# Expert stage of an attention-and-experts kernel: row numbers in one read, placements together, fetches ahead of the dense stores

## The chip, the cores and the metric

The kernel runs on one core of one Trainium2 chip. Its time is the device time of one execution in microseconds (us). Before the change three runs gave 252.63, 248.10 and 251.63; their median is 251.63.

## The reference

Block-sparse attention is followed by a mixture of experts on its result. What the last stage must compute:

```python
x = attn_out.transpose(0, 2, 1, 3).reshape(B * S, H * D)   # 3072 tokens x 512
y_dense = np.maximum(x @ w1_dense, 0.0) @ w2_dense
logits = x @ w_gate                                          # 8 experts
expert_idx = np.argmax(logits, axis=1)
...
gate_w = probs[np.arange(N), expert_idx]
for e in range(E):
    mask = expert_idx == e
    h = np.maximum(x[mask] @ w1[e], 0.0)
    y_moe[mask] = gate_w[mask, None] * (h @ w2[e])
return y_dense + y_moe
```

There are 4 batches of 8 heads with 768 positions, so 3072 tokens; each token goes to the one expert with the largest logit, and every token also gets the dense product.

## The kernel before

The attention part takes two heads at a time over 16 steps. When a batch of 768 tokens is done, `batch_fills` makes its later work: transposes (`xtr`), the logits and gate weights (`gate`), each token's slot (`ranks`), the placement of the tokens (`place`), and the dense product in 28 pieces (`l1` and `l2`). For the first three batches this is spread between the attention steps of the next batch. The last batch has no attention behind it, so its pieces are spread by hand over the first blocks of the expert stage.

Placing means that GpSimd (POOL) writes 128 tokens, each as a row of 544 two-byte values (the token, its gate weight and its number), into the DRAM tensor `table` at the rows that `ranks` found: six indirect DMAs for a batch (line 360). `table` has a range of rows for each expert, so a block of 128 tokens of one expert is 128 rows in sequence.

There are two lists of blocks. The first (N1 = 11 blocks, 0 to 10) is made when three batches are counted and holds only tokens of these. The second (20 blocks, 11 to 30) is made by `lists` after the last batch is counted, and holds the rest. A list gives each block its expert (`eo`, an offset into the weights) and its first row in `table` (`ro`). Both are read into registers by `registers` (line 435): SyncE (SP) needs `ro` to fetch rows, TensorE (PE) and VectorE (DVE) need `eo` to find the weights. The last three blocks are under a condition and are rarely run, so the loop goes over 28 blocks (0 to 27).

For a block the work is:

- `fetch` (line 456): SP reads 128 rows of `table` into a tile `xg`; there are 14 such tiles, so a fetch from block 14 on waits until the block 14 earlier has been used up, its scatter included.
- `own` (line 471): DVE copies the expert's first weights out of a big tile.
- `tx` (lines 815 and 817): PE transposes the rows, DVE copies them out of PSUM.
- `e1` (lines 824 and 827): the first product, and ScalarE (ACT) applies the ReLU.
- `e2` (lines 845, 852, 853): the second product, ACT multiplies by the gate weight into one of five tiles `yo`, and POOL adds it to the output rows with an indirect DMA. Here it is called the block's scatter. For block 27 POOL reads the dense rows first (`dense_rows`, line 837), DVE adds, and the scatter writes the sum.

The dense product's results are stored to the output by SP in two halves for every 128 tokens (line 403). A scatter must come after the dense store of the same tokens. For blocks of the first list the kernel declares that they hold no token of the last batch, so their scatters wait only for the earlier batches' dense stores; the scatters from block 11 on wait for all of them.

Each engine works its instructions off in order. In what order the instructions of one engine stand is decided by the order in the code and by a scheduler; `tc.issue_after` asks that something be put behind a given instruction. SP's queue of the last stage holds fetches, dense stores, the reads of `ro`, and `empty`: eight writes of zero rows behind each expert's tokens (line 868), whose row numbers are read at line 864.

In the loop, `extra` says which pieces of the last batch are made at which block: `gate` and `ranks` at block 0, placement t at block 1 + t, the clearing writes at block 3, the 28 dense pieces over blocks 1 to 9. `AHEAD` and `READY` bound how far fetches are asked for ahead: the first list's as soon as eight ahead, the second's three for each block from block 8 on, each behind the latest dense store that has been issued.

Of the kernel before, what the change touches and what calls it, by code (L numbers as in the profile page):

```python
# [17 lines left out]
def kernel(  # L18
# [14 lines left out]
    NT = S // 128  # L33
# [9 lines left out]
    NBLK = NM + E - 1  # L43
# [13 lines left out]
    N1 = (N * (B - 1) // B - E * 127 + 127) // 128  # L57
# [41 lines left out]
    latest = {}  # L99
# [53 lines left out]
    N1R = -(-N1 // 4) * 4  # L153
# [77 lines left out]
    def apart(dma, group, reason):  # L231

        if group in groups:
            tc.declare_no_dep(dma.ins, group=group, reason=reason)
        groups.add(group)
        tc.add_to_no_dep_group(group, dma.ins)
# [195 lines left out]
    rows = []  # L432

    def registers(src, engine, top, why):
        _, v = nc.values_load_multi_w_load_instructions(src, engines=[engine], min_val=0, max_val=top,  # L435
                                                        skip_runtime_bounds_check_because=why,
                                                        bass_reorder=False)
        return v

    def load_offs():  # L440

        k = len(offs)
        n, c = (min(4, N1 - k), k) if k < N1 else (min(10, NBLK - k), k - N1 + N1R)
        for have, engine in ((offs, mybir.EngineType.PE), (offs1, mybir.EngineType.DVE)):
            have.extend(registers(eo[:, c : c + n], engine, (E - 1) * NK * 512,
                                  "the expert of a block is at most the last"))

    def load_rows(n):
        rows.extend(registers(ro[:, len(rows) : n], mybir.EngineType.SP, EMPTY,
                              "blocks lie in their expert's rows, or are the empty one"))  # L450
# [3 lines left out]
    def fetch(i):  # L454
        es[i]["x"] = xg = eg.tile([128, XW], U16, name="xg")
        ld = nc.sync.dma_start(out=xg, in_=table[bass.ds(rows[i], 128)])
        if i < N1:
            tc.add_to_no_dep_group("full", ld.ins)
# [5 lines left out]
    def own(i):  # L464
        if i < 1:
            w = eg.tile([128, NK, 512], HF, name="w1a", bufs=1)
        else:
            w = later[0].tile([128, NK, 512], HF, name="w1", bufs=2)
        es[i]["w1"] = w
        with tc.issue_after(latest["xT"].ins) if "xT" in latest else nullcontext():  # L470
            nc.vector.tensor_copy(w.rearrange("p j f -> p (j f)"), w1f[:, bass.ds(offs1[i], NK * 512)])  # L471

    FIRST = 6
    with (
# [251 lines left out]
        for i, (p, u) in enumerate(seq):  # L726
# [59 lines left out]
            if p == NP - 2 and u == 8:  # L786
                load_rows(N1)
                load_offs()
# [9 lines left out]
    with (  # L798
# [8 lines left out]
        a, d, ranks, places, _ = batch_fills(B - 1)  # L807
# [3 lines left out]
        def tx(i):  # L811
            s = es[i]
            tp = p1.tile([128, NK, 128], HF, name="tp", tag="tr")
            for ko in range(NK):
                nc.tensor.transpose(tp[:, ko], s["x"][:, ko * 128 : (ko + 1) * 128].bitcast(HF), ident)  # L815
            s["xT"] = xT = et.tile([128, NK, 128], HF, name="exT")
            latest["xT"] = nc.vector.tensor_copy(xT, tp)  # L817

        def e1(i):
            s = es[i]  # L820
            hp = p2.tile([128, NK, 128], FP, name="hp", tag="h")
            for j in range(NK):
                for ko in range(NK):
                    nc.tensor.matmul(hp[:, j], s["w1"][:, ko, j * 128 : (j + 1) * 128], s["xT"][:, ko],  # L824
                                     start=(ko == 0), stop=(ko == NK - 1), skip_group_check=True)
            s["hT"] = h = et.tile([128, NK, 128], HF, name="ehT")
            nc.scalar.activation(h, hp, AF.Relu)  # L827

        def tokens(i):
            return bass.IndirectOffsetOnAxis(ap=es[i]["x"][:, Dm + 2 : Dm + 4].bitcast(mybir.dt.int32), axis=0)  # L830

        def dense_rows(i):

            es[i]["dense"] = dr = et.tile([128, Dm], FP, name="dr", bufs=1)
            nc.gpsimd.memset(dr, 0.0)
            with tc.issue_after(latest["pool"].ins):
                ga = nc.gpsimd.indirect_dma_start(out=dr, out_offset=None, in_=out, in_offset=tokens(i),
                                                  bounds_check=N - 1, oob_is_err=False)
            apart(ga, "add", "every token is in one block")

        def e2(i):
            s = es[i]
            yp = p3.tile([128, Dm], FP, name="yp", tag="y")
            for j in range(NK):
                nc.tensor.matmul(yp, s["hT"][:, j], w2f[:, bass.ds(offs[i] + j * 512, 512)],  # L845
                                 start=(j == 0), stop=(j == NK - 1))
            o = et.tile([128, Dm], FP, name="yo", bufs=5)
            gate, to = s["x"][:, Dm : Dm + 2].bitcast(FP), tokens(i)
            if "dense" in s:
                nc.vector.scalar_tensor_tensor(o, yp, gate, s["dense"], ALU.mult, ALU.add)  # L850
            else:
                nc.scalar.mul(o, yp, gate)  # L852
            sc = nc.gpsimd.indirect_dma_start(out=out, out_offset=to, in_=o, in_offset=None, bounds_check=N - 1,  # L853
                                              oob_is_err=False,
                                              compute_op=ALU.bypass if "dense" in s else ALU.add)
            latest["pool"] = sc
            apart(sc, "add", "every token is in one block")
            if i < N1:
                tc.declare_no_dep(sc.ins, group="dense", reason="the first blocks hold no token of the last batch")
                tc.add_to_no_dep_group("add1", sc.ins)  # L860
# [9 lines left out]
                tc.declare_no_dep(z.ins, group="full", reason="the first blocks end before these rows")  # L870

        AHEAD = 8
        READY = 8
        for i in range(1, 1):
            own(i)
        tx(0)
        extra = {0: a[:NT] + [a[NT], ranks], **{1 + t: [f] for t, f in enumerate(places)}}
        extra[3].append(empty)
        for n, f in enumerate(d):
            extra.setdefault(1 + n * (N1 - 2) // len(d), []).append(f)  # L880
        got = FIRST

        RARE = 3
        NOFT = NBLK - RARE
        for i in range(NOFT):
            if i > 2 and len(rows) < NBLK:
                load_rows(min(len(rows) + 4, NBLK))
            while got < min(i + AHEAD + 1, NOFT, N1 + 3 * max(i - READY + 1, 0)):
                if got < N1:
                    fetch(got)  # L890
                else:
                    with tc.issue_after(latest["ys"].ins):
                        fetch(got)
                got += 1
            if 1 <= i + 1 < NOFT:
                own(i + 1)
            e1(i)
            if i + 1 < NOFT:
                tx(i + 1)
            for f in extra.get(i, ()):  # L900
                f()
            if i > 0:
                e2(i - 1)
            if len(offs) < min(i + 4, NBLK):
                load_offs()
            if i == NOFT - 6:
                dense_rows(NOFT - 1)
            if i == READY + 1:
                total = nc.values_load_multi_w_load_instructions(
                    nblk, min_val=0, max_val=N2, bass_reorder=False,  # L910
                    skip_runtime_bounds_check_because="the blocks that are left are at most N2")[1][0]
# [39 lines left out]
```

## Time and profile before

| | us |
|---|---|
| median of the three runs | 251.63 |
| lowest and highest | 248.10, 252.63 |
| the profiled execution, its own time | 250.08 |
| its span | 248.4 |
| PE busy (share of the span) | 207.8 (84%) |
| DVE busy | 176.2 (71%) |
| ACT busy | 174.4 (70%) |
| POOL busy | 161.6 (65%) |

The mean granted clock of PE is 0.984. In the profile, "q" behind an engine's name is its sequencer, which waits, branches, reads registers and issues DMAs; these are not counted as busy. Times in the timeline count from the span's start. In a row of the timeline stand the start, the length, the engine, the line, the operation, the output and inputs by name, the number of instructions merged, and in brackets the idle time before it with what ended it. A wait for several things is put down to the one that came last by the profile; where that had long been done, it was another. The last 7.5 us are the last scatter and the end of the program, so what matters in this stage is when the last scatter can start.

### The profile page before, as it was taken

To read this page: it belongs to the slowest core of one execution; us is meant where nothing else is said; L and a number is where in the kernel's file an instruction comes from. 1 tells how busy PE (TensorE), PEld (TensorE's weight loads), DVE (VectorE), ACT (ScalarE), POOL (GpSimd) and SP (SyncE) were. 2 spreads that over 40 slices of the span, in tenths; PEclk is the share of its full clock that TensorE was granted. 3 is DMA by queue.
4 is the path that set the end of the run, shared out by engine and by line. 5 is a ranking of instruction groups with operands and counts; after the bars stand their busy time and mean duration, and the time that the engine had idled before them with its cause. 6 is when DMAs were issued, how large, how long until landed. Compare 5 with 4: busy or idle time off the path is not lost. (4 is left out here: it accounts for less than half of the span.)

```text
span 248.4 us, 7579 instructions
## 1 busy us (share of the span) xinstructions
PE 207.8 (84%) x2771; PEld 148.7 (60%) x2771; DVE 176.2 (71%) x555; ACT 174.4 (70%) x325; POOL 161.6 (65%) x199
## 2 busy tenths in 40 slices
PE   1688878888998999988999998989999869979930
PEld 0466555666665676756667765667666557757710
DVE  3889999989989789797798998588423135545410
ACT  5589788878787898696899787815656636646620
POOL 6457997586289677268977427603888543888881
PEclk9999999999999999999999999999999999999985
DMA  7999999999999999989999966167599999977785
GB/s 181 252 254 253 208 226 255 253 205 261 226 180 348 192 295 233 203 176 222 304 190 256 222 116 180 62 163 213 123 267 210 162 245 228 195 133 102 123 118 104
DMA packets 75446, 50.54 MB, mean 204 GB/s; under 512 B 29712, under 2 KB 68496, under 8 KB 75408
## 3 DMA queue, kind: packets, MB, share of 16 engines
q1 hardware_dynamic: 60176, 30.72, 48.1%
q0 software_dynamic: 15232, 19.32, 46.5%
q8 instruction: 23, 0.38, 0.6%
q14 instruction: 15, 0.12, 0.2%
HBM read 41.93 MB, written 18.23 MB: 242 GB/s over the span
## 5 line engine op out<-in xcount | busy, mean ns | idle before, releaser
L567 ACT ACTIVATE ex<-sp 128x512 f16<-128x512 f32 (+1 forms) x176 | 91.5, 607 | 10.5 <-PE sp L563 8.1
L563 PE MATMUL sp<-rT,kT 128*128 128x128 f16 (+3 forms) x384 | 63.9, 261 | 3.6 <-ACT ex L567 1.2
L853 POOL DMA_INDIRECT out_dram<-yo,xg x28 | 44.8, 1600 | 26.0 <-DMA xg<-table 13.1
L569 POOL TENSOR_SCALAR_AFFINE_SELECT ex<-ex 128x512 f16<-128x512 f16 x48 | 32.3, 686 | 34.9 <-ACT ex L567 32.2
L582 PE MATMUL op<-v,ex 128*128 128x65 f16 x672 | 45.5, 194 | 7.4 <-POOL ex L569 5.3
L582 PEld LDWEIGHTS <-ex 128*128 128x128 f16 x672 | 35.6, 98 | 22.5 <-POOL ex L569 9.7
L817 DVE COPY exT<-tp 128x512 f16<-128x512 f16 x28 | 11.9, 424 | 33.2 <-PE tp L815 27.4
L563 PEld LDWEIGHTS <-kT 128*128 128x128 f16 x384 | 28.3, 98 | 7.4 <-issue 4.4
L824 PEld LDWEIGHTS <-w 128*128 128x128 f16 x432 | 26.3, 98 | 8.2 <-issue 2.9
L360 POOL DMA_INDIRECT table<-xbig,slot x24 | 24.9, 1038 | 9.4 <-issue 9.1
L824 PE MATMUL hp<-exT,w 128*128 128x128 f16 x432 | 29.2, 219 | 1.8 <-issue 1.8
L852 ACT ACTIVATE yo<-yp,xg 128x512 f32<-128x512 f32 x27 | 18.6, 687 | 15.0 <-PE yp L845 14.6
L845 PE MATMUL yp<-we,ehT 128*128 x112 | 28.9, 379 | 0.3 <-ACT ys L400 0.2
L379 PE MATMUL hp<-xT,wd 128*128 128x384 f16 x128 | 28.6, 325 | 0.6 <-DVE xT L248 0.6
L505 DVE TENSOR_REDUCE ks<-kp 128x24 f16<-128x768 f16 x28 | 25.5, 946 | 3.7 <-ACT kp L501 3.5
L827 ACT ACTIVATE ehT<-hp 128x512 f16<-128x512 f32 x28 | 16.7, 597 | 14.8 <-PE hp L824 11.3
L395 PE MATMUL yp<-wd,hT 128*128 128x512 f16 x96 | 25.9, 379 | 0.3
L384 ACT ACTIVATE hT<-hp 128x384 f16<-128x384 f32 x30 | 15.0, 499 | 9.5 <-PE hp L379 9.0
L471 DVE COPY w<-we 128x2048 f16 x27 | 19.5, 724 | 1.8 <-PE hp L824 1.7
L593 DVE TENSOR_TENSOR xbig<-op,rs 128x384 f16<-128x384 f32 x32 | 17.5, 548 | 0.9 <-DVE rs L591 0.7
L400 ACT COPY ys<-yp 128x512 f32<-128x512 f32 x21 | 12.8, 607 | 6.2 <-PE yp L395 6.2
L493 POOL CAST v<-vf 128x768 f16<-128x768 f32 x16 | 13.4, 840 | 4.2 <-DMA vf<-in_v_dram 3.0
(149 smaller groups left out, 364.1 us busy)
## 6 DMA issues: line engine op xcount, KB each, us to landing
we<-in_moe_w_dram POOLq DMA_DIRECT2D x16, 512.0 KB, 7.7
kf<-in_k_dram SPq DMA_DIRECT2D x32, 192.0 KB
qf<-in_q_dram SPq DMA_DIRECT2D x32, 192.0 KB
vf<-in_v_dram SPq DMA_DIRECT2D x32, 192.0 KB
out_dram<-ys SPq DMA_DIRECT2D x48, 128.0 KB
xg<-table SPq DMA_DIRECT2D x28, 136.0 KB
table<-zt SPq DMA_DIRECT2D x9, 136.0 KB
wd<-in_moe_w_dense_dram POOLq DMA_DIRECT2D x2, 512.0 KB, 8.8
```

What stands on the lines that cost most here:

```text
L360: sc = nc.gpsimd.indirect_dma_start(out=table, out_offset=bass.IndirectOffsetOnAxis(ap=keep["slot"][:, t : t + 1], axis=0), in_=xbig[b % 2 ...
L379: nc.tensor.matmul(hp, wd[:, ko, j * 128 : (j + 1) * 128], xT[:, ko, g * G * 128 : (g + 1) * G * 128], start=(ko == 0), stop=(ko == NK - 1))
L395: nc.tensor.matmul(yp, hold["h"][:, j, i * 128 : (i + 1) * 128], wd[:, NK + j], start=(j == 0), stop=(j == NK - 1))
L471: nc.vector.tensor_copy(w.rearrange("p j f -> p (j f)"), w1f[:, bass.ds(offs1[i], NK * 512)])
L505: nc.vector.tensor_reduce(out=ks[:, i], in_=kp.rearrange("d (c w) -> d c w", w=32), op=op, axis=mybir.AxisListType.X)
L563: last = nc.tensor.matmul(sp[:, o : o + w], kT[p % NB][g][:, kt * 128 : (kt + 1) * 128], rT[p % NB][g][:, a * 128 : z * 128], start=(o == ...
L567: scored.append((last, nc.scalar.activation(ex[:, 0:o], sp[:, 0:o], AF.Exp, scale=-0.125)))
L569: latest["pool"] = nc.gpsimd.affine_select(out=ex, in_=ex, compare_op=ALU.is_ge, fill=0.0, base=0, pattern=[[0, 4], [1, 2], [2, 64]], chan ...
L582: nc.tensor.matmul(s["op", g][:, t * (D + 1) : (t + 1) * (D + 1)], ex[:, o : o + 128], v16[p % NB][:, g, kt, :], start=first, stop=(last_o ...
L824: nc.tensor.matmul(hp[:, j], s["w1"][:, ko, j * 128 : (j + 1) * 128], s["xT"][:, ko], start=(ko == 0), stop=(ko == NK - 1), skip_group_che ...
L845: nc.tensor.matmul(yp, s["hT"][:, j], w2f[:, bass.ds(offs[i] + j * 512, 512)], start=(j == 0), stop=(j == NK - 1))
L853: sc = nc.gpsimd.indirect_dma_start(out=out, out_offset=to, in_=o, in_offset=None, bounds_check=N - 1, oob_is_err=False, compute_op=ALU.by ...
```

## The change

Six edits, all in the expert stage:

- `load_rows`: the 20 row numbers of the second list are read by one instruction at block 3, not four at a time from block 3 on.
- `load_offs`: the second list's expert offsets are read four at a time, not ten.
- the placements of the last batch are made by threes at blocks 2 and 3, not one for each of blocks 1 to 6.
- the results (`e2`) of blocks 0 and 1 come ahead of the pieces in `extra` (gate, ranks, dense pieces, placements) at blocks 1 and 2, not behind them.
- `READY` is 7, not 8, so fetches of the second list are asked for a block sooner, and they are no longer put behind the latest dense store.
- the spread of the dense pieces is written with 9 in place of N1 - 2, which is the same number.

```diff
@@ load_offs
-        n, c = (min(4, N1 - k), k) if k < N1 else (min(10, NBLK - k), k - N1 + N1R)
+        n, c = (min(4, N1 - k), k) if k < N1 else (min(4, NBLK - k), k - N1 + N1R)
@@ expert stage
-        READY = 8
+        READY = 7
...
-        extra = {0: a[:NT] + [a[NT], ranks], **{1 + t: [f] for t, f in enumerate(places)}}
-        extra[3].append(empty)
+        extra = {0: a[:NT] + [a[NT], ranks]}
+        for t, f in enumerate(places):
+            extra.setdefault(2 + t // 3, []).append(f)
+        extra.setdefault(3, []).append(empty)
         for n, f in enumerate(d):
-            extra.setdefault(1 + n * (N1 - 2) // len(d), []).append(f)
+            extra.setdefault(1 + n * 9 // len(d), []).append(f)
...
             if i > 2 and len(rows) < NBLK:
-                load_rows(min(len(rows) + 4, NBLK))
+                load_rows(min(len(rows) + 20, NBLK))
             while got < min(i + AHEAD + 1, NOFT, N1 + 3 * max(i - READY + 1, 0)):
-                if got < N1:
-                    fetch(got)
-                else:
-                    with tc.issue_after(latest["ys"].ins):
-                        fetch(got)
+                fetch(got)
                 got += 1
             if 1 <= i + 1 < NOFT:
                 own(i + 1)
             e1(i)
             if i + 1 < NOFT:
                 tx(i + 1)
+            if 0 < i < 3:
+                e2(i - 1)
             for f in extra.get(i, ()):
                 f()
-            if i > 0:
+            if i >= 3:
                 e2(i - 1)
```

## The prediction

> **What bounds the kernel now.** I read the chain of work that ended last first, then the timeline of each engine from 150 us on. All edits lie in the last stage, blocks 0 to 27 (line 824 on, from 164 us). Blocks 0 to 10 are from the first list, 11 to 27 from the second. "Scatter n" is block n's POOL instruction that adds its result into the output (line 853).
>
> ```profile
> 190.06 2.01 SPq L435
> ...
> 195.02 1.77 SPq L435
> ...
> 197.07 3.58 DMA xg<-table
> ...
> 200.70 0.40 PE tp L815 x4
> ```
>
> The columns are start, length, what. In the middle of the stage the chain is neither PE nor POOL: SP reads row numbers into registers (line 435) four at a time, and the fetch of block 11 stands behind these reads.
>
> ```profile
> 197.07 1.06 PE L824 MATMUL hp<-exT,w 128*128 128x128 f16 x16
> 200.70 0.40 PE L815 MATMUL tp<-ident,xg 128*128 128x128 f16 x4 [2.58 <-DMA xg<-table]
> 204.89 1.03 PE L845 MATMUL yp<-we,ehT 128*128 x4
> ...
> 206.87 1.03 PE L845 MATMUL yp<-we,ehT 128*128 x4
> ...
> 219.20 1.05 PE L824 MATMUL hp<-exT,w 128*128 128x128 f16 x16 [1.41 <-issue]
> 205.96 0.69 ACT L852 ACTIVATE yo<-yp,xg 128x512 f32<-128x512 f32 x1 [0.43 <-PE yp L845]
> ```
>
> The timeline of PE and, last, of ACT: PE waits 2.58 us for block 11's rows, then makes a block every 1.98 us (204.89 to 206.87). Block 11's result is ready at 205.96 + 0.69 = 206.65.
>
> ```profile
> 171.62 2.25 POOL L853 DMA_INDIRECT out_dram<-yo,xg  x1 [9.01 <-DMA xg<-table]
> ...
> 177.28 1.60 POOL L853 DMA_INDIRECT out_dram<-yo,xg  x1 [0.30 <-issue]
> ...
> 188.87 1.34 POOL L360 DMA_INDIRECT table<-xbig,slot  x1 [0.30 <-issue]
> ...
> 192.39 1.61 POOL L853 DMA_INDIRECT out_dram<-yo,xg  x1 [0.30 <-issue]
> ...
> 198.23 1.55 POOL L853 DMA_INDIRECT out_dram<-yo,xg  x1 [1.74 <-ACT yo L852]
> ...
> 210.50 1.64 POOL L853 DMA_INDIRECT out_dram<-yo,xg  x1 [3.81 <-DMA xg<-table]
> ...
> 231.85 1.07 POOL L837 DMA_INDIRECT dr<-out_dram,xg  x1 [0.30 <-issue]
> ...
> 242.61 1.03 POOL L853 DMA_INDIRECT out_dram<-yo,xg  x1 [0.31 <-issue]
> ```
>
> These rows are scatters 0 and 1, the sixth placement, scatters 6, 8 and 11, the gather for block 27, and scatter 27. From 210.50 to 242.61 POOL rests only 0.30 between instructions, so **the end is the start of scatter 11 plus 32.11 us of POOL**, plus 7.47 to the profiled execution's 250.08 us (span 248.4). Scatter 11 starts 3.85 us after its result is ready. Its rows had landed at 197.07 + 3.58 = 200.65, so the fetch that is named was long done: it is the first scatter that may touch tokens of the last batch, so it waits for all dense stores of line 403.
>
> ```profile
> 168.59 2.50 SPq L456 DMA_DIRECT2D xg<-table  x5
> ...
> 178.32 0.35 SPq L456 DMA_DIRECT2D xg<-table  x1
> 178.87 5.86 SPq L868 DMA_DIRECT2D table<-zt  x6
> 184.83 8.47 SPq L403 DMA_DIRECT2D out_dram<-ys  x6
> 197.07 1.45 SPq L456 DMA_DIRECT2D xg<-table  x3
> ...
> 202.89 3.17 SPq L403 DMA_DIRECT2D out_dram<-ys  x4
> L403 SPq DMA_DIRECT2D out_dram<-ys x18: 467/572/1356, 162.0 to 204.7; - x18
> ```
>
> SP's timeline and the summary of line 403 (least, median, most ns; first and last start): the last store begins at 204.7, and scatter 11 follows 5.8 us later. So SP holds up both PE (2.58) and POOL (3.85).
>
> **The change part by part.** In the changed order of instructions the six placements stand in one row on POOL, behind scatter 1; both fetches of blocks 9 and 10 precede them; SP has one read of 20 row numbers behind five of the eight clearing writes; fetches 11 to 19 precede the last three dense results' stores, and fetch 20 stands between the first and the other two of these.
>
> *Fetch 10.* Today (178.32) it waits for a placement. Then it follows the five fetches that end at 168.59 + 2.50 = 171.1, and all that follows on SP moves up.
>
> ```profile
> SPq L456 <- DMA table<-xbig,slot: 5.0, 1, 5.0
> 175.33 0.21 DVE L345 TENSOR_SCALAR ro<-rs,h 1x20 int32<-1x20 f32 x1
> L435 SPq TENSOR_LOAD <-ro x5: 1645/2006/2754, 181.6 to 195.0; - x5
> L864 SPq TENSOR_LOAD <-zo x1: 537/537/537, 171.5 to 171.5; - x1
> L435 PEldq TENSOR_LOAD <-eo x5: 529/1513/2881, 149.6 to 216.3; - x5
> ```
>
> The first row, of SP's waits, gives back 5.0 us. The row numbers are written at 175.54, so the read starts near 175.7.
>
> *The read of 20.* No row shows one. Below: 0.54 (line 864, eight registers). Above: five reads at the worst, 5 x 2.754 = 13.8. Nearest by size is PE's read of ten at 2.88 (at 216.3), twice that is 5.8; five medians are 10.0. I take 7.
>
> The Trainium skill (Runtime: NRT & Kernel Launch, section Instruction fetch mechanics) gives about 200 ns for each register, even in bulk: by it 20 registers are an estimated 4.0 us and one step saves nothing. The trace agrees with neither side of it: 67 ns each in line 864's read, 411 to 689 in the reads of four.
>
> *SP after the read.* Three clearing writes at 0.55 and six stores at 0.57 are 5.1 us; nine fetches (three took 1.45 with their gaps, so 0.57 with the next gap), a 0.3 read and two stores are 6.6. So fetch 20 can go at 175.7 + read + 11.7: 194.4 with a read of 7.
>
> *Placements.* Placements stood between scatters 0 and 1; now scatter 1 waits only for its result, which comes before six dense products that stood ahead of it.
>
> ```profile
> 161.97 2.07 DMA out_dram<-ys
> ...
> 171.96 1.01 PE hp L379 x6
> 172.97 0.86 PE yp L845 x4
> ```
>
> The chain's last two rows here give 172.97 + 0.86 - 1.01 = 172.8; with ACT's 0.69 and some 0.2 between, scatter 1 starts near 173.7, not 177.28, and the row of placements, after 1.60 and a short copy, near 175.8. The first row is a dense store's landing.
>
> ```profile
> L360 POOL DMA_INDIRECT table<-xbig,slot x6: 974/1095/1505, 174.2 to 188.9; - x6
> L360 POOL DMA_INDIRECT table<-xbig,slot x6 | 7.0, 1168 | 1.8 <-issue 1.5 <-DVE rs L339 0.3
> DMA to landing us min/median/max: 4.1/4.4/4.6
> DMA to landing us min/median/max: 4.3/5.2/6.1
> 193.99 0.69 ACT L852 ACTIVATE yo<-yp,xg 128x512 f32<-128x512 f32 x1 [1.11 <-PE yp L845]
> ```
>
> The placements by least, median and most; their sum and mean; the landings of placements and of scatters; ACT's write of block 7. Six at 1.17 + 0.30 are 8.8 us (bounds by least and most: 7.6 and 10.8). The last begins near 183.1 instead of 188.87 and lands near 187.5, and fetch 11 goes near 187.8: block 11's rows are there by 191.4, PE wants them near 198, and **the 2.58 us are gone** (only a start after 194.3 brings them back; a 13.8 read gives 194.6, 0.3 late). Scatters 2 to 6 are pushed back: scatter 2 at 184.6, scatter 6 at 184.6 + 4 x 1.9 = 192.2, as now. Each result has five buffers, so block 7's write waits for scatter 2's landing, 189.8, against its 193.99 now (the last row): covered by 4 us. Scatters 7 on wait for PE as now (scatter 8 waited for ACT).
>
> *Fetch 20 and the last stores.* Its buffer comes free when scatter 6 lands, 192.2 + 5.5 = 197.7 (5.2 to 6.1). That fetch and three stores later the last store begins, near 200.2, not 204.7. After 5.8 us, as now, scatter 11 would go at 206.0; with a landing of 2.07 at 202.3. PE gives the floor: 206.65 - 2.58 + 0.27 (scatter 8 follows its result by that) = 204.3. I take the middle of floor and upper end, 205.15, since the fetches that crowd the stores today are over by then.
>
> The Trainium skill (DMA: Bandwidth & Descriptors, section Anatomy of one DMA) fits a software-issued DMA as 2.0 us plus bytes over 436 GB/s, an estimated 2.6 us for a scatter of 256 KB. By it fetch 20 would go 2.9 us sooner and PE's floor would decide, 0.85 less in the sum. The rows of this case, 4.3 to 6.1, speak against it.
>
> *Reads of expert offsets.* Ten at once become four at once, five reads each on PE and DVE in place of two; all start on a multiple of four, like the shortest of PE's now (0.53). The 1.41 us at 219.20 stand behind a read of 2.88, so PE's queue covers about 1.5; reads under that are free. Above: 2.06 (three registers on PE, off the multiple), 0.5 each. I take nothing. Without this PE would be the later one after scatter 11.
>
> *Results 0 and 1 ahead.* Same PE work in another order: gate and ranks slip by 0.2 us, hidden by PE's own order. Nothing.
>
> **Sum.** Scatter 11 moves from 210.50 to 205.15, POOL's 32.11 stay (up to the gather POOL takes 231.85 - 210.50 = 21.35, PE ten blocks at 1.98 and a scatter of 1.93, 21.7; from PE's floor of 204.3 that ends at 236.8, below), so scatter 27 starts at 237.26 and the profiled execution becomes 237.26 + 7.47 = 244.73. The three runs shown lie around their own mean of 250.79, 0.71 above the profiled 250.08 (median 251.63): the forecast is **245.4**, 5.4 us or 2.1% under that mean. Its own range goes with scatter 11 from 204.3 to 206.0 and half a microsecond for POOL: 244.6 to 246.4.
>
> **The rivals.**
> *SP still decides.* If the read takes over 10.3 us, fetch 20 and the stores slip by the rest: at 13.8, 3.5 us, scatter 11 at 208.65 to 209.5, time 248.9 to 249.7. For it: the reads of four sum to over 10. Against it: ten registers in 2.88.
>
> *The row of placements clogs POOL (slower).* Six scattered writes in a row may be held back until earlier ones land, 4.4 us, instead of 1.47. Scatters 2 to 6, fetch 20, the last stores and scatter 11 then all slip by six times the excess. From 2.4 each scatter 11 is back at 210.5; at 3.4, halfway, it comes near 216.7 and the time is 257. For it: scatter 0 took 2.25. Against it: today's mixed row runs on with 0.30 gaps, and
>
> ```profile
> 185.00:190.00 5.00, 5.00 (x46) 3.21 (x44) 2.12 (x4) 3.09 (x6) 4.08 (x4) 1.00 1.03 210
> ```
>
> the DMA engines' share there (second last) is 1.03 while POOL issues on (4.08 of 5).
>
> **How the numbers follow.** Forecast 0.70, SP 0.18, clog 0.12. Two per cent is about what a measurement of this kernel can tell. Of the forecast 0.64 is faster by over 2%, of SP's case 0.03: 0.67; slower is the clog, 0.12; the rest, 0.21, is within. The range goes down to the fastest run shown less the gain, 248.1 - 5.4 = 242.7, less 0.6 for a start at PE's floor, 242.1; up to SP's upper end, 249.7. It leaves out the clog and a little of the rest.
>
> **What would show it.** Right: no wait of PE for block 11's rows; one SP read at 175 to 176 of under 10 us; scatter 11 at 204 to 206; 32 us from it to scatter 27. Wrong: placements over 2 us each, a last store after 204, or PE waiting behind line 435.

## Result and profile after

The changed kernel takes 253.35 us (median of 20 runs, 251.58 to 262.26), the kernel before 252.64 in 20 runs beside it. The ratio is 1.0108, interval 1.0069 to 1.0148: no change at the 2% that the forecast spoke of, and rather 1% slower than 2% faster. The profiled execution took 254.62 us (span 252.9). Its first product of block 0 starts at 167.59 us, not at 164.04, so below many times are counted from that product ("after the first product"). Profiles marked * in the table further down are of executions that took longer than most others of the same kernel, and what only they show is left open.

The summary of line 435 (least, median, most in ns) and POOL's timeline, with scatter 1, the first and the last placement, and scatters 2, 11 and 27:

```profile
L435 PEldq TENSOR_LOAD <-eo x8: 330/498/1271, 152.7 to 235.3; - x8
L435 SPq TENSOR_LOAD <-ro x2: 1917/4000/6082, 154.5 to 179.1; - x2
```

```profile
177.57 1.57 POOL L853 DMA_INDIRECT out_dram<-yo,xg  x1 [1.55 <-DVE w L471]
...
180.00 1.00 POOL L360 DMA_INDIRECT table<-xbig,slot  x1 [0.28 <-POOL xbig L354]
...
186.44 0.97 POOL L360 DMA_INDIRECT table<-xbig,slot  x1 [0.30 <-issue]
187.72 1.60 POOL L853 DMA_INDIRECT out_dram<-yo,xg  x1 [0.30 <-issue]
...
214.16 1.57 POOL L853 DMA_INDIRECT out_dram<-yo,xg  x1 [0.30 <-ACT yo L852]
...
246.88 1.03 POOL L853 DMA_INDIRECT out_dram<-yo,xg  x1 [0.30 <-issue]
```

The read of 20 takes 6.08 us and the six placements follow each other by 1.29. Scatter 11 nevertheless starts at 214.16 - 167.59 = 46.57 after the first product, where the kernel before had 210.50 - 164.04 = 46.46. SP's timeline tells why the stores could not be early, PE's, ACT's and DVE's why the result was not:

```profile
188.59 4.31 SPq L403 DMA_DIRECT2D out_dram<-ys  x6
193.16 11.23 SPq L456 DMA_DIRECT2D xg<-table  x9
204.49 1.11 SPq L403 DMA_DIRECT2D out_dram<-ys  x2
206.03 0.34 SPq L456 DMA_DIRECT2D xg<-table  x1
206.47 2.42 SPq L403 DMA_DIRECT2D out_dram<-ys  x4
```

```profile
184.96 1.02 PE L845 MATMUL yp<-we,ehT 128*128 x4 [0.55 <-issue]
...
190.85 1.02 PE L845 MATMUL yp<-we,ehT 128*128 x4 [2.89 <-ACT yo L852]
190.12 0.69 ACT L852 ACTIVATE yo<-yp,xg 128x512 f32<-128x512 f32 x1 [5.20 <-remote]
190.30 0.43 DVE L817 COPY exT<-tp 128x512 f16<-128x512 f16 x1 [5.69 <-remote]
```

Fetches 11 to 19 alone hold the queue for 11.23 us, and the last store begins 40.7 us after the first product, just where the kernel before had it (204.7 - 164.04), not at 36.2 (200.2 - 164.04) as forecast. And ACT takes up block 3's product at 190.12 although PE's matmuls for it ended at 184.96 + 1.02 = 185.98 by the records: the signal came 4.1 us late, ACT and DVE stood, and then PE waited 2.89 for ACT. From block 5 on the results come 6.5 to 6.7 us later after the first product than in the second profile below, and scatter 11 follows its own result by the usual 0.3. (The last store of this page begins at 208.3.)

A second profile of the same kernel (`after_again`) has no such stop. ACT's write of result 11, and scatter 11, with SP's rows:

```profile
205.58 0.69 ACT L852 ACTIVATE yo<-yp,xg 128x512 f32<-128x512 f32 x1 [0.43 <-PE yp L845]
...
213.28 1.83 POOL L853 DMA_INDIRECT out_dram<-yo,xg  x1 [6.96 <-DMA xg<-table]
...
190.05 11.45 SPq L456 DMA_DIRECT2D xg<-table  x9
201.61 1.12 SPq L403 DMA_DIRECT2D out_dram<-ys  x2
202.97 1.04 SPq L456 DMA_DIRECT2D xg<-table  x1
204.12 3.34 SPq L403 DMA_DIRECT2D out_dram<-ys  x4
```

Here result 11 is ready at 206.27, 39.5 after the first product (42.6 before), a gain of 3 us as forecast. It then lies for 7.0 us. The last store begins at 206.86 and lands at 212.36; scatter 11 starts at 213.28, 46.54 after the first product. The row names a fetch, but block 11's fetch is from 190.05, so the store is taken as what it waits for. Two profiles, two different last waits, one result. That pointed to something behind both.

### The profile page after: what moved, and what is told of

It is laid out like the page before. It is cut to its first block, busy times and chain, and to the rows that moved or that the text cites. A ratio compares the mean times of both kernels' runs of the same rounds, so it can differ in the third digit from the quotient of the medians.

```text
span 252.9 us, 7581 instructions
## 1 busy us (share of the span) xinstructions
PE 212.4 (84%) x2771; PEld 152.0 (60%) x2771; DVE 173.8 (69%) x555; ACT 173.5 (69%) x325; POOL 160.6 (63%) x199
## 4 chain that ended last, share of the span: by engine, by line
DMA 21%; POOL 21%; PE 16%; DVE 14%; issue 12%; ACT 6%; SPq 5%; another core or an unknown queue 2%; POOLq 1%; DVEq 0%; ACTq 0%
POOL out_dram L853 9%; DMA vf<-in_v_dram 9%; DVE ks L505 5%; DMA out_dram<-yo,xg 4%; DMA qf<-in_q_dram 4%; POOL table L360 3%; POOL ex L569 3%; PE sp L563 3%; ACT ex L567 2%; DMA xg<-table 2%; PE hp L379 2%; PE hp L824 2%; PE op L582 2%; ACT kp L501 2%
## 5 line engine op out<-in xcount | busy, mean ns | idle before, releaser
L563 PE MATMUL sp<-rT,kT 128*128 128x128 f16 (+3 forms) x384 | 64.9, 263 | 3.1 <-DVE rT L683 0.7
L853 POOL DMA_INDIRECT out_dram<-yo,xg x28 | 43.6, 1556 | 28.0 <-ACT yo L852 14.4
L582 PE MATMUL op<-v,ex 128*128 128x65 f16 x672 | 46.3, 196 | 7.6 <-POOL ex L569 6.2
L582 PEld LDWEIGHTS <-ex 128*128 128x128 f16 x672 | 36.4, 99 | 23.1 <-POOL ex L569 11.0
L563 PEld LDWEIGHTS <-kT 128*128 128x128 f16 x384 | 28.7, 99 | 7.3 <-issue 4.2
L824 PEld LDWEIGHTS <-w 128*128 128x128 f16 x432 | 27.1, 99 | 7.8 <-issue 2.5
L824 PE MATMUL hp<-exT,w 128*128 128x128 f16 x432 | 30.1, 222 | 1.2 <-ACT hT L384 0.7
L360 POOL DMA_INDIRECT table<-xbig,slot x24 | 24.2, 1009 | 9.4 <-issue 8.8
L471 DVE COPY w<-we 128x2048 f16 x27 | 18.7, 694 | 0.2 <-PE hp L824 0.2
L845 PEld LDWEIGHTS <-ehT 128*128 128x128 f16 x112 | 10.1, 98 | 11.9 <-issue 4.7
```

Of the source, the lines that this page charges most:

```text
L360: sc = nc.gpsimd.indirect_dma_start(out=table, out_offset=bass.IndirectOffsetOnAxis(ap=keep["slot"][:, t : t + 1], axis=0), in_=xbig[b % 2 ...
L563: last = nc.tensor.matmul(sp[:, o : o + w], kT[p % NB][g][:, kt * 128 : (kt + 1) * 128], rT[p % NB][g][:, a * 128 : z * 128], start=(o == ...
L582: nc.tensor.matmul(s["op", g][:, t * (D + 1) : (t + 1) * (D + 1)], ex[:, o : o + 128], v16[p % NB][:, g, kt, :], start=first, stop=(last_o ...
```

## Experiments

Theory S: scatter 11 is late because the last dense stores stand on SP's queue behind fetches 11 to 20. Rival D: between some 20 us after the first product and scatter 11 the DMA engines are full, so that an order only chooses who waits. After the second group of runs a third suspect was added, the late signals of PE. All runs by their numbers (us after the first product; "PE wait" is for block 11's rows; "DMA" is the engines' share from 20 to 44 us; it passes 1 in places, so it is no exact share of time):

```
run               ratio to before            result 11  scatter 11  PE wait  DMA   stage
before (page)                                  42.60      46.45      2.58    1.00  84.3
before_again                                   40.64      46.03      -       1.02  84.0
d_before          0.9988 [0.9946, 1.0030]      41.82      47.02      -       0.99  85.8
after (page)      1.0108 [1.0069, 1.0148]      46.21      46.56      -       0.96  85.3
after_again       1.0111 [1.0045, 1.0176]      39.53      46.54      -       1.05  85.1
a_spread          1.0117 [1.0063, 1.0170]      44.97      47.08      3.09    0.97  84.5
a_rows4           1.0086 [1.0047, 1.0124]      40.55      47.33      -       0.99  85.7
b_late            1.0022 [0.9975, 1.0068]      45.56      46.05      -       0.90  84.3
b_ready7          1.0033 [1.0002, 1.0065]      45.86      46.21      -       0.92  85.2
b_early *         1.0122 [1.0083, 1.0162]      41.91      49.50      -       0.98  88.2
b_store12         1.0032 [0.9992, 1.0072]      46.12      46.47      -       0.95  84.9
c_late *          1.0153 [1.0082, 1.0224]      46.21      47.82      -       0.88  87.5
c_store12         1.0136 [1.0054, 1.0218]      46.72      47.07      -       0.94  85.5
c_late_rows4      1.0101 [1.0030, 1.0172]      46.02      46.37      -       0.84  84.7
c_late_spread *   1.0023 [0.9948, 1.0099]      42.28      45.04      0.57    0.99  82.5
d_store12_spread  1.0092 [1.0058, 1.0126]      47.81      48.16      4.06    0.97  87.1
d_threes *        none                         47.35      47.71      -       0.94  86.5
d_late_twos       0.9928 [0.9876, 0.9980]      42.82      46.68      0.33    0.96  84.9
e_late_twos *     1.0048 [0.9998, 1.0097]      45.52      45.88      3.16    0.97  84.3
e_last *          0.9960 [0.9906, 1.0015]      46.96      47.31      4.25    0.92  85.7
```

**First group: the kernels again, and single edits undone.** `after_again` and `before_again` are the two kernels unchanged. `a_spread` undoes the placements by threes, `a_rows4` the read of 20:

```diff
# a_spread
-            extra.setdefault(2 + t // 3, []).append(f)
+            extra.setdefault(1 + t, []).append(f)
# a_rows4
-                load_rows(min(len(rows) + 20, NBLK))
+                load_rows(min(len(rows) + 4, NBLK))
```

> The changed kernel once more, nothing edited. In its first profile ACT stood idle from 184.92 to 190.12 and DVE from 184.61 to 190.30 although PE's products for them were there by 186 to 187; without these 5 us scatter 11 would start 41 us after the first block's product, as forecast, and not 46.6. If the stop belongs to the change, it is here again, 15 to 20 us after the first block's product, and scatter 11 starts 46 to 47 us after it. If it was a chance of that execution, it is gone, scatter 11 starts at 41 to 42, and the time is 0.98 of the kernel before in this execution; then the 1.01 over many runs needs another cause.

> The kernel before once more, nothing edited, to see how much two executions of it differ. If the attention part's length is chance (it was 164.04 before and 167.59 after, with the same instructions), this run's first block's product lies anywhere from 162 to 168; the stage from there to the end is 84.4 as before, give or take 0.5, and there is no stop of all engines in it.

> The changed kernel with the last batch's placements one by one at blocks 1 to 6, as before; all else as changed. Theory A (six placements in a row bring on the stop of all engines): no stop, time 0.98 of before. Theory B (SP's single read of 20 row numbers, 6 us, brings it on): the stop is still there, just behind that read, and the time stays near 1.01. Theory C (chance): as the changed kernel.

> The changed kernel with the second list's row numbers read four at a time, as before; all else as changed. Theory A (placements in a row): the stop is still there, time near 1.01 of before. Theory B (the single read of 20): no stop and the time 0.98 to 0.985. Theory C (chance): as the changed kernel.

None of these profiles has the stop, `after_again` with both suspects and `a_rows4` with the six placements included, so neither A (the placements) nor B (the read) makes it alone; and the changed kernel whose profile lacks the stop is still at 1.0111, not at 0.98. With the placements spread, fetch 11 starts at 32.2 us and PE waits 3.09 for its rows: it is the placements, not the read, that set fetch 11. They do it by way of SP, where fetch 10 waits for a placement again (the waits from 170 to 178 us of `a_spread`):

```profile
SPq L456 <- DMA table<-xbig,slot: 5.3, 1, 5.3
```

Without the read of 20 nothing is lost: fetch 11 at 25.2 us instead of 23.3, still in time. And `before_again` has no wait of PE for block 11's rows at all, yet its scatter 11 starts at 46.03. So the 2.58 us of the page before were a matter of that execution, and taking them away is worth nothing.

**Second group: the order of stores and fetches.** `b_late` puts the dense stores back in their former places, `b_ready7` half way, `b_early` gives the kernel before only the change's place for them, and `b_store12` takes the last ones off the queue altogether: the first three results of the last batch are stored twice, ahead of fetch 11, and the last three are not stored, so the traffic stays and the dense product of the last 384 tokens is missing.

```diff
# b_late (b_ready7: the second part alone)
-        READY = 7
+        READY = 8
...
-                fetch(got)
+                if got < N1:
+                    fetch(got)
+                else:
+                    with tc.issue_after(latest["ys"].ins):
+                        fetch(got)
# b_early: the same two parts the other way round, in the kernel before
# b_store12
-                for j in range(NJ):
+                for m, j in [(m + G * r, j) for r in range(2) for j in range(NJ)] if b == B - 1 and g == 0 else [] if b == B - 1 else [(m, j) for j in range(NJ)]:
```

> The changed kernel, with the dense results' stores put back where the kernel before has them: ready at block 8 and bound to issue after their result is written, so that six stores stand ahead of fetch 11 and the rest are threaded between the fetches of blocks 11 to 20. Theory S (the last stores are late because they stand behind fetches 11 to 20, and scatter 11 waits for their landing): the last store begins 2 to 4 us earlier than the 40.12 us after the first block's product that the changed kernel showed, scatter 11 starts at 41 to 44 us instead of 46.5, and the stage from the first product to the end takes 80 to 83 us instead of 85. Ratio to before 0.975 to 0.995. Rival D (the DMA engines are full from 24 to 48 us whatever the order): scatter 11 at 45 us or later, the stage 84 us or longer, ratio 1.00 to 1.015.

> The changed kernel, with only the binding of each dense store to the write of its result put back (ready at block 7 as in the change). Six stores then stand ahead of fetch 11, two behind fetch 16 and four behind a later one. S: one or two fetches less stand ahead of the last stores than in the changed kernel, scatter 11 at 42 to 46 us after the first product, ratio 0.985 to 1.01. D: scatter 11 at 45 us or later, ratio 1.00 to 1.015.

> The kernel before with one part of the change alone: dense results ready at block 7, their stores not bound to the write of the result. Fetches 11 to 19 then stand ahead of two more stores and fetch 20 ahead of the last four, while the rows' numbers are still read by the former single steps. S: the last stores begin later than the 40.66 us of the kernel before, scatter 11 at 47 to 49 us instead of 46.0 to 46.5, ratio 1.005 to 1.02. D: the traffic is that of before, scatter 11 at 46 to 46.5, ratio 0.995 to 1.005.

> The changed kernel, with the stores of the last three dense results taken off the queue behind the fetches: the first three results of the last batch are stored twice instead, the second time to the rows of the last three, so that all twelve stores stand ahead of fetch 11 and the traffic in bytes and transfers is the same. The dense product of the last 384 tokens is thereby left out of the output. S: nothing that scatter 11 waits for is behind the fetches any more, it starts with its result, at 39.5 to 41.5 us after the first product, the stage takes 78 to 80 us, ratio 0.97 to 0.985. D: the same bytes have to pass, scatter 11 still starts at 45 us or later, ratio 1.00 to 1.015.

`b_early` came out as S says, 1.2% slower: stores behind more fetches do cost. Its result 11 is ready at 41.91 and the scatter waits until 49.50:

```profile
216.89 1.56 POOL L853 DMA_INDIRECT out_dram<-yo,xg  x1 [7.55 <-DMA xg<-table]
```

D had 46 to 46.5 and a ratio of at most 1.005 for this run, and falls there: with the same traffic, the order alone made the kernel slower. The other three did not come out as S says. In `b_late`, `b_ready7` and `b_store12` scatter 11 no longer waits for a store, but its result comes 6 us later than in `after_again`. The timeline of `b_store12`, ACT and POOL:

```profile
188.38 0.69 ACT L852 ACTIVATE yo<-yp,xg 128x512 f32<-128x512 f32 x1 [5.26 <-remote]
...
212.24 1.57 POOL L853 DMA_INDIRECT out_dram<-yo,xg  x1 [0.30 <-ACT yo L852]
```

It is the stop of the page after again, in the same place. In these three S was neither borne out nor ruled out: one wait had taken the place of the other.

**Third group: what makes the stop.** `c_late` and `c_store12` repeat `b_late` and `b_store12`; `c_late_rows4` is `c_late` without the read of 20, `c_late_spread` is `c_late` with placements one by one (diffs as above).

> The same kernel as in the run b_late: the changed kernel with the stores of the dense results back in their former places. In its first profile scatter 11 followed its own result at once (46.05 after 45.56 us from the first product), but TensorE had lost 4.1 us before: VectorE and ScalarE stood from 17.3 to 22.5 us for a signal of TensorE whose matmuls had ended 4.1 us before by the records, which the first profile of the changed kernel had shown too and a second one had not. S (stores behind fetches): where that stop is absent, result 11 is ready at 40 to 41.5 us and scatter 11 starts within 1.5 us of it, stage 79 to 81 us, ratio 0.975 to 0.99; where it is present, as in b_late, ratio about 1.00. D (the DMA engines full whatever the order): scatter 11 at 45 us or later without the stop as well, ratio 1.00 to 1.015.

> The same kernel as in the run b_store12: all twelve stores ahead of fetch 11, the last three dense results' own stores left out and the first three of the last batch stored twice (the dense product of the last 384 tokens is not in the output). S: without the stop of TensorE's signals, scatter 11 starts with its result at 40 to 42 us after the first product, ratio 0.97 to 0.985; with it ratio about 1.00. D: scatter 11 at 45 us or later also without the stop, ratio 1.00 to 1.015.

> As c_late, but the second list's row numbers read four at a time, as the kernel before reads them. If the long read of 20 numbers is what holds TensorE's signals back between 11 and 22 us, no stop shows here whether or not c_late has one, and the time lies up to 4 us under that of c_late; if it is not, the stop is here whenever c_late has it. By S the reads of four (1.3 to 1.7 us each in the earlier run with them) delay the fetches by less than their lead, ratio 0.975 to 0.995 without a stop; D 1.00 to 1.01.

> As c_late, but the last batch's rows placed one by one between the blocks, as in the kernel before. If six placements back to back are what holds TensorE's signals back, no stop shows here whether or not c_late has one; if the long read does, the stop is here as in c_late. Without a stop, fetch 11 waits for the last placement and begins near 32 us after the first product, so that TensorE waits 2 to 3 us for block 11's rows as in the kernel before; ratio 0.995 to 1.01.

`c_late` has a ratio of 1.0153 where the same kernel as `b_late` had 1.0022, and their intervals don't meet; `c_store12` has 1.0136 where `b_store12` had 1.0032. From one group to another a ratio moves by 1% and more than its interval says, so ratios are compared within a group only.

The stop is there without the read of 20 (`c_late_rows4`, ACT's write of block 3):

```profile
191.57 0.69 ACT L852 ACTIVATE yo<-yp,xg 128x512 f32<-128x512 f32 x1 [5.13 <-remote]
```

and it is not there with placements spread. So it goes with six placements in a row, not with the long read. But it does not come from them alone: `after_again` and `a_rows4` have the same row of placements and no stop: over blocks 0 to 11 ACT, when free, starts 0.04 to 0.11 us after PE's last matmul by the records (one start of `a_rows4`, 0.86, apart). The profiles fall into two kinds. In the page before, the first group and the fifth they hold some 5,700 semaphore events, and signals come within 0.11 us as said. In the page after and the second to fourth groups they hold 4,763 to 4,947, and over the same blocks the latest signal is 4.05 to 4.23 us late in all seven profiles with six placements in a row, 0.67 to 1.08 late in the four with single ones. The kernel before is slower in the second to fourth groups too (median 251.88 to 252.38, against 248.62 in the first and 250.62 in the fifth), though its page, with some 5,700 events, belongs to 20 runs with a median of 252.64. The first and the third group ran on the same chip. What the condition is stays open.

**Fourth group: both suspects away.** `d_before` is the kernel before once more. `d_store12_spread` is `b_store12` with placements one by one. `d_threes` puts a scatter between the two threes, `d_late_twos` is `b_late` with placements by twos and a scatter between the pairs:

```diff
# d_threes and d_late_twos
-            if 0 < i < 3:
+            if 0 < i < 4:
...
-            if i >= 3:
+            if i >= 4:
# d_late_twos, beside the parts of b_late
-            extra.setdefault(2 + t // 3, []).append(f)
+            extra.setdefault(1 + t // 2, []).append(f)
```

> The kernel before itself, for a profile beside the others of this group. If the stop of TensorE's signals belongs to six placements back to back, it shows no stop over 1.5 us between 10 and 24 us after the first product; if it belongs to the chip's state in these runs whatever the kernel, it shows one of 4 us here too. Ratio 0.995 to 1.005, stage about 84 to 85 us.

> The changed kernel with both suspects taken away: all twelve stores ahead of fetch 11 (the first three results of the last batch stored twice, the last three results' own stores left out, so that the dense product of the last 384 tokens is not in the output), and the placements one by one between the blocks. S (scatter 11 waits for stores behind fetches, and the packed placements cost the stop): no stop, scatter 11 within 1 us of its result, at 40 to 42.5 us after the first product, stage 78 to 81 us, ratio 0.975 to 0.99. D (the DMA engines are full and set the time of scatter 11): scatter 11 at 45 us or later, or TensorE waiting 2 us and more for block 11's rows in its place, stage 84 us or longer, ratio 1.00 or more.

> The changed kernel with the second result too ahead of the last three placements, so that the six placements come as three, a scatter, three, instead of six in a row. If the run of six is what makes the stop, it is gone or under 2 us here; if any dense group of placements does, it stays at 4 us. The dense stores still stand behind the fetches, so by S scatter 11 stays at 45 to 47 us and the ratio at 1.005 to 1.015 in both cases.

> Both repairs together with the correct output: the dense stores in their former places (as b_late) and the placements two at a time with a scatter between the pairs. S: no stop over 2 us, fetch 11 at 24 to 28 us, TensorE does not wait for block 11's rows, scatter 11 at 42 to 45 us, stage 80.5 to 83 us, ratio 0.98 to 0.995, which would beat both kernels. If pairs still make the stop: scatter 11 at 46 us, ratio 1.00 to 1.01. D: scatter 11 at 45 us or later without a stop, ratio 1.00 or more.

`d_store12_spread` has no stop and no store behind a fetch. Its timeline of SP, PE and POOL, and a wait of SP between 170 and 202 us:

```profile
189.22 11.41 SPq L403 DMA_DIRECT2D out_dram<-ys  x12
200.87 7.52 SPq L456 DMA_DIRECT2D xg<-table  x11
...
206.33 0.40 PE L815 MATMUL tp<-ident,xg 128*128 128x128 f16 x4 [4.06 <-DMA xg<-table]
...
214.28 1.56 POOL L853 DMA_INDIRECT out_dram<-yo,xg  x1 [0.30 <-ACT yo L852]
...
SPq L456 <- DMA table<-xbig,slot: 6.1, 1, 6.1
```

The twelve stores now take the place that fetch 11 had, PE waits 4.06 us for block 11's rows, and scatter 11 starts at 48.16, later than in any other run but `b_early`. Stores first, rows late; rows first, stores late. D had named this outcome. S had 40 to 42.5, and that number fell; its mechanism did not, for scatter 11 follows its result by 0.35. Nor is the run a clean test of S: with single placements SP loses 6.1 us at fetch 10 ahead of all twelve stores, as it lost 5.3 in `a_spread`, where PE waited 3.09 with only six stores ahead. No run has early placements, all stores ahead and no stop at once. `d_before` has no stop although its profile is of the kind with fewer events, no wait of PE, and scatter 11 at 47.02, 5.2 us after its result. `d_threes` lies between: ACT's latest signal is 1.95 us late and DVE still stands for 6.9 us (its median was 254.23 against 251.88; there is no ratio). `d_late_twos` is the first changed kernel whose ratio lies under 1, with a latest signal 1.52 us late, result 11 at 42.82 and the scatter 3.9 us behind it:

```profile
200.38 2.93 SPq L456 DMA_DIRECT2D xg<-table  x3
203.41 3.13 SPq L403 DMA_DIRECT2D out_dram<-ys  x4
...
202.04 0.40 PE L815 MATMUL tp<-ident,xg 128*128 128x128 f16 x4 [0.33 <-PE hp L824]
...
211.84 1.64 POOL L853 DMA_INDIRECT out_dram<-yo,xg  x1 [3.81 <-DMA xg<-table]
```

**Fifth group: the last four stores alone.** `e_late_twos` is `d_late_twos` again; `e_last` moves its last four stores ahead of fetches 14 to 16 and nothing else:

```diff
-            while got < min(i + AHEAD + 1, NOFT, N1 + 3 * max(i - READY + 1, 0)):
+            while got < min(i + AHEAD + 1, NOFT, N1 + 3 * max(i - READY + (i == READY), 0)):
```

> The same kernel as in the run d_late_twos, beside the next one on one chip: ratio 0.985 to 1.00. Scatter 11 at 46 to 47 us after the first product, 3.5 to 4.5 us after its result, since the last four stores stand behind fetches 14 to 16 and begin 3 to 4 us after the last dense result is written.

> As d_late_twos, but fetches 14 to 16 come after the last four stores on SyncE's queue; nothing else changes its place. S (scatter 11 waits for stores behind fetches): the last four stores begin at 34.5 to 37.5 us instead of 38.25 to 40.26, scatter 11 starts at 42.5 to 44.5 us instead of 46.7, block 14's rows still come in time (a wait of TensorE of 1 us at most), stage 81.5 to 83.5 us, ratio 0.975 to 0.99, under that of the kernel beside it. D (the DMA engines are full until 46 us in any order): the stores land as late as before though they begin earlier, scatter 11 at 45.5 us or later, or TensorE waits over 1.5 us for block 14's rows; ratio as beside it.

In `e_last` the last four stores begin at 37.7 to 39.6 instead of 39.2 to 41.0, and scatter 11 waits for none of them; but PE waits 4.25 us for block 11's rows in that execution and 3.16 in `e_late_twos`, and scatter 11 starts at 47.3 and 45.9. Side by side `e_last` is the faster by medians, 250.45 against 251.47, with ratios of 0.9960 and 1.0048 whose intervals meet; neither interval leaves out 1. `d_late_twos` was 0.9928 on one chip and the same kernel 1.0048 on another. Both profiles of this group are marked *, so what the order of the last four stores is worth stays open, and no version here is shown to beat the kernel before.

**The rival that is left.** The windows from 20 to 44 us after the first product; the last two figures of a row are the DMA engines' share and GB/s. Before, `after_again`, `d_store12_spread`:

```profile
184.04:208.04 24.00, 21.18 (x222) 14.70 (x223) 8.42 (x16) 13.12 (x23) 14.65 (x10) 1.00 1.00 210
```

```profile
186.74:210.74 24.00, 23.76 (x259) 16.85 (x257) 9.70 (x19) 15.48 (x26) 14.94 (x10) 1.00 1.05 243
```

```profile
186.12:210.12 24.00, 18.85 (x172) 12.68 (x171) 5.72 (x12) 11.32 (x20) 12.31 (x9) 0.94 0.97 228
```

PE's busy time goes from 18.85 to 23.76 of the 24 us, the DMA engines' stays at 0.97 to 1.05. Summed over the packets from the first product to scatter 11, the 16 engines are busy for 39 to 44 us of the 45 to 49.5 in every one of the 20 profiles (8.8 to 10.1 MB). The shares under 0.95 belong to runs in which PE's signals stood, and to `e_last`. Scatter 11 was moved by no edit to under 45 us, which is what D says. But D is not shown. `b_early` speaks against its strong form: an order can cost 3 us with the same traffic. At shares near 1 the engines moved 210 GB/s before and 243 in `after_again`, so the share is no fixed ceiling in bytes. And in the first 10 us of the stage it is 0.68 to 0.80, so there is room earlier. SP's own queue is another rival: in `after_again` it goes from store to fetch to store with hardly a gap from 19.3 to 40.7 us (waits for buffers within the fetches counted in), and every order so far has kept the same instructions in it. A run that takes traffic away, or spreads these instructions over two queues, would decide; none was made.

## Why the prediction was wrong

The fourth point below rests on three rows of `after_again`: SP's waits while fetches 11 to 19 are issued (190 to 201.6 us), the landing of scatter 5, and the landing of the last store.

```profile
SPq L456 <- DMA out_dram<-yo,xg: 4.8, 3, 2.5
...
DMA to landing us min/median/max: 7.6/7.6/7.6
...
DMA to landing us min/median/max: 5.5/5.5/5.5
```

- **PE's wait for block 11's rows goes: right, and worth nothing.** Fetch 11 started 23.3 us after the first product in `after_again` (forecast 187.8, which is 23.8), and PE did not wait. But the kernel before had no such wait in two of its three profiles, and scatter 11 stood at 46.0 and 47.0 in them.
- **The read of 20: right.** 7 us assumed, 6.08 and 5.94 measured in the two profiles, 5.4 to 6.9 over all runs with it; PE shows no wait behind line 435 in them. The Trainium skill (Runtime: NRT & Kernel Launch, section Instruction fetch mechanics) had given an estimated 4.0; the measured 270 to 347 ns for each register is above its 200.
- **Placements: right in their own time** (1.29 each, forecast 1.47). The rival of a clogged POOL did not come. What came in some groups of runs, a stop of PE's signals of 4 us beside the six placements, was not thought of.
- **"Fetch 20 and the last stores": the step that failed.** It had the last store begin at 200.2, 36.2 after the first product; it began at 40.1 in `after_again` and 40.7 in the page after. Scatter 6 was in time there (28.7, forecast 28.2). But fetch 19, which the step did not look at, had to wait for scatter 5, and that landed 7.6 us after its start (26.7 to 34.3), where 5.5 was assumed for scatter 6. The two stores, fetch 20 and four stores behind it then went at 0.95 each (34.4 to 40.1), where 0.57 was assumed. Of the 5.4 us by which scatter 11 was missed there (46.54 for 41.11), 4.0 are this; 0.6 are the step from the last store's start to the scatter (6.4 for 5.8), and 0.85 come from taking the middle and not the upper end. In the page after the last store is as late, and the stop, which the prediction does not have, makes the result as late as the scatter. The landing's size was taken from scatters of the page before, and the reason "the fetches that crowd the stores today are over by then" was wrong: fetches 11 to 20 run until 204.0, 37.3 after the first product, and the DMA engines' share is 0.96 to 1.05 from 20 to 44 us in the two profiles, as in the kernel before (0.99 to 1.02). Why landings and issues stretched stays open between D and SP's queue. By the Trainium skill (DMA: Bandwidth & Descriptors, section Anatomy of one DMA) a scatter would have been an estimated 2.6 us: the trace moved still further from it.
- **The floor of 204.3 by PE** holds in `after_again`: its result 11 was ready at 39.5, 40.3 minus the usual 0.27 is 40.0. It was the stores, not PE, that decided, and when they were put first it was the result again, late by the stop or by block 11's rows.
- **The 32.11 us from scatter 11 to 27: nearly right**, 246.88 - 214.16 = 32.72. The end after it is 254.62 - 246.88 = 7.74, forecast 7.47.
- **The base.** The forecast's own range has a small slip: 204.3 to 206.0 gives 244.6 to 246.3, and the half microsecond for POOL is not in it. The forecast stood on three runs with a mean of 250.79; 20 runs of the same kernel have a median of 252.64. Of the 7.95 us by which the forecast missed, 1.85 are that, and the range ended under the time of the unchanged kernel.

What stays open is the size of the loss. The stage takes 85.1 and 85.3 us in the two profiles of the changed kernel, 84.0, 84.3 and 85.8 in those of the kernel before; 1.1% of the time would be 2.7 us. The rest lies ahead of the stage, where no instruction was changed: 166.7 and 167.6 us against 163.6 to 165.0. Most of it is one wait of POOL for the values' load, in the waits between 42 and 58 us of `after_again`, and of the kernel before:

```profile
POOL v L493 <- DMA vf<-in_v_dram: 3.8, 1, 3.8
```

```profile
POOL v L493 <- DMA vf<-in_v_dram: 1.4, 2, 1.0
```

Other versions with the same change begin the stage early (`a_rows4`: at 163.5, with 1.8 us of this wait), so it may be chance; five profiles can't tell.

## What to carry to other kernels

When a fetch is moved forward, ask for each fetch on its queue, not only for the last, what frees its buffer and when that lands: here fetch 19's wait for scatter 5 held the stores behind it. When a queue is full from end to end, and the DMA engines' share stands near 1 beside it, expect that a fetch moved forward is a store moved back, and that the wait changes its name and keeps its length, until a run shows otherwise. Look at a second profile of the unchanged kernel before a wait is counted as a gain: here the 2.58 us were in one of three. And take the spread of the runs of before into the base of the range, not only into its edges.

## What was not expected of the hardware

- In some groups of runs PE's signals reach ACT late, by 4.05 to 4.23 us beside six indirect placements in a row (seven profiles) and by 0.67 to 1.08 beside single ones (four profiles); in other groups by no more than 0.11 with the same code (but for one start at 0.86). PE's next matmuls are on record as run in the meantime.
- A number read into a register took 0.27 to 0.35 us in the reads of 20, 0.32 to 0.43 in the reads of four of `a_rows4`, and 0.41 to 0.69 in the same reads of the page before; over all six profiles with reads of four it is 0.22 to 0.72. One long read takes 5.4 to 6.9 us, five medians of four 7.7 in `a_rows4` and 10.0 in the page before.
- In `after_again` an accumulating scatter of 128 x 512 values landed 7.6 us after its start, against the 4.3 to 6.1 of the prediction's row; the DMA engines' share was 1.08 from 26 to 35 us after the first product.
